# The lower part of a split weight tile, computed by GpSimd instead of VectorE (delta-rule attention feeding a softplus MLP)

## The chip, the core and the metric

The kernel runs on one core of one Trainium2 chip. The metric is the device time of one execution in microseconds; where several executions were timed, their median. The profiled execution is one of its own, with its own time. Engine names in the profile's rows: PE is TensorE (PEld its weight loads), DVE is VectorE, ACT is ScalarE, POOL is GpSimd, SP is SyncE, which here only issues DMAs.

## What is computed

Two layers, one after the other. The first is a delta-rule linear attention over 768 steps, for 4 batches of 8 heads with head size 48; the second a feed-forward layer over the resulting 3072 tokens, 384 -> 2048 -> 384, with a softplus between the two weight matrices:

```python
for t in range(S):                       # attention, per batch b and head h
    y[:, :, t] = einsum('bhd,bhde->bhe', q[:, :, t], state)
    v_old = einsum('bhde,bhd->bhe', state, kt)
    state = state + bt * einsum('bhd,bhe->bhde', kt, vt - v_old)
...
h = x @ w_in                             # feed-forward, x is y as 3072 x 384
g = maximum(h, 0) + log1p(exp(-abs(h)))
return g @ w_out
```

All inputs and outputs are float32, except that the weights arrive as 64-bit floating point words, read as pairs of 32-bit integers.

## The kernel before, in words

The sequence is cut into 12 steps of 64 positions (`NS`), and all 32 heads go through a step together. A step of the attention forms the Gram matrix of its keys, inverts a triangular system (`invert`, `finish`, `join`, `cross_a`, `arrange`, `cross_b`), and then gives the output of the step and the new state (`k_state`, `p_half`, `u_all`, `y_all`, `state`). The inverse is prepared for two steps at a time: `invert` is a long row of small VectorE instructions on the tiles Z, ltq and work (lines 199 to 229), `finish` transposes the result into the tile tt (lines 235 and 236), `join` (line 246 and behind) multiplies with tt, and `arrange` copies a part of tt (line 275) and clears it (line 277, a GpSimd memset).

The feed-forward layer (`moe`) follows one step behind: the 256 tokens of step s are called chunk s here. A chunk goes through the 16 column tiles f of the hidden layer in pairs. For a pair, TensorE multiplies the tokens with the first weights into ph (line 465), ScalarE computes Abs, Exp and Ln (469 to 471), VectorE puts the softplus together, and TensorE adds the pair's product with the second weights to po (line 448), one pair late: `late` holds that product back until the next pair's ph has been issued. ph has two buffers.

The precision differs by chunk. Chunk 0 uses plain float32 weights. From chunk 1 on every operand is split into an upper part in the type fp32r and a lower part, the difference to it, and three products are added (`TERMS`: upper x upper, upper x lower, lower x upper). The softplus is then made by three VectorE instructions: line 473 (its inputs are ph in PSUM and a in SBUF), line 475 (a cast, the upper part gh) and line 476 (a subtraction, the lower part gl).

The weights are prepared once. `weights` (lines 382 to 411) turns the 64-bit words into float32 with four VectorE instructions a tile (396, 399, 403, 406) and a ScalarE copy (409) into HF[f]. `split` (lines 413 to 419) then makes the two parts, once for each of the 16 tiles of 128 x 768 elements, and is called in chunk 1 just ahead of the pair that needs them: a ScalarE copy of HF[f] into hf, a tile from the three buffers of "ex" (line 416); a ScalarE cast of hf to the upper part w[:, 0] (line 418); and the difference of the two into the lower part w[:, 1] (line 419). W[f] has the place of HF[f]. The next user of an "ex" buffer waits until line 419 has read it.

The order on each engine is fixed when the program is built. The prologue's order is written out by hand (`manual_schedule`); after it a scheduler decides, from the order of the code and its own estimates of durations, in which order each engine gets its instructions. At run time every engine works its list in that order, and waits on semaphores for what it needs. SP's list of DMAs is not touched by what follows.

Of the kernel before, what the change touches and what calls it, by code (L numbers as in the profile page):

```python
# [12 lines left out]
ALU = mybir.AluOpType  # L13
# [22 lines left out]
def deltanet_moe(ctx, tc, kT, qT, kN, kI, vN, beta, wts, out):  # L36
    nc = tc.nc
# [375 lines left out]
    def split(f):  # L413

        hf = two.tile([P, 2 * DM], F32, name="ex", bufs=3)
        nc.scalar.copy(hf, HF[f])
        w = W[f] = one.tile([P, 2, 2 * DM], F32R, name=f"w{f}")
        nc.scalar.copy(w[:, 0], hf)
        nc.vector.tensor_tensor(w[:, 1], hf, w[:, 0], op=ALU.subtract)  # L419


    def moe():
# [4 lines left out]
        for s in range(NS):  # L427
# [26 lines left out]
            for f0 in range(0, NF, 2):  # L454
                while done[0] < f0 + 2:
                    next(conversion)
                if s == 1:
                    for f in range(0 if f0 == 0 else f0 + 2, min(f0 + 4, NF)):
                        split(f)
# [320 lines left out]
```

## Time and profile before

| | |
|---|---|
| runs of the kernel before | 673.43 us median of 3 (671.69 to 679.93) |
| the profiled execution | 672.51 us, of which 670.8 us is the span from its first to its last instruction |
| granted TensorE clock, mean | 0.971 |
| busy of the span | PE 91%, PEld 85%, DVE 67%, ACT 56%, POOL 5% |
| line 419, the instruction that moves | 16 times on DVE, 124.9 to 168.9 us, 15.1 us in all |

The span falls into three parts. Up to about 120 us come the loading of inputs, the first inverses and the conversion of the weights. From there to about 190 us chunk 1 runs, with the 16 splits in it. Behind that, 10 more chunks run with everything at hand, and TensorE works nearly without a break. Line numbers in rows (L419) are those of the code above; out<-in are the names of tiles, buffer numbers left out; "idle ... <-" names what ended the idle time just before the instruction.

### The profile page before, as it was taken

What the parts mean: (1) busy time and instruction counts of PE and PEld (TensorE: products, weight loads), DVE (VectorE), ACT (ScalarE), POOL (GpSimd) and SP (SyncE); (2) the same over time, 40 slices, a digit from 0 to 9 for tenths busy, and PEclk for the clock granted to TensorE, in tenths of its full rate; (3) what the DMA queues carried; (4) which work ended last, traced back from release to release, by engine and by line L of the source; (5) the groups of instructions that cost most, each with busy time, mean ns of one, the idle gap of its engine ahead of it and who ended that gap; (6) DMA issues with size and microseconds to landing.
All of it is one profiled execution on the core that took longest, in us unless ns stands there. A gap on an engine that the chain in (4) does not pass through costs nothing.

```text
span 670.8 us, 24090 instructions
## 1 busy us (share of the span) xinstructions
PE 612.4 (91%) x10736; PEld 571.7 (85%) x10736; DVE 451.9 (67%) x970; ACT 372.5 (56%) x687; POOL 30.5 (5%) x56
## 2 busy tenths in 40 slices
PE   4456968899888999989999999999999999999997
PEld 3455756579888999988999999998999998999997
DVE  4966498978555985556997558985539984544443
ACT  4334767879664447464456555555554546454433
POOL 3200010000000001000001000001000001000000
PEclk9998977899998999999999999997999998999999
DMA  9837286000140120140210322200302100200000
GB/s 232 271 98 207 64 262 150 0 25 4 52 108 26 48 61 26 50 108 27 70 38 28 81 78 71 61 25 21 90 4 71 38 24 5 60 25 13 2 23 23
DMA packets 35095, 44.80 MB, mean 67 GB/s; under 512 B 21776, under 2 KB 27184, under 8 KB 34992
## 3 DMA queue, kind: packets, MB, share of 16 engines
q1 hardware_dynamic: 34992, 43.27, 22.9%
q8 instruction: 84, 1.38, 0.9%
q14 instruction: 19, 0.16, 0.1%
HBM read 36.27 MB, written 4.72 MB: 61 GB/s over the span
## 4 chain that ended last, share of the span: by engine, by line
PE 77%; ACT 8%; DVE 7%; issue 5%; DMA 2%; POOL 1%; SPq 0%; ACTq 0%; DVEq 0%; POOLq 0%
PE ph L465 29%; PE po L448 27%; PE pa L345 4%; PE pa L304 3%; PE pa L330 2%; PE pa L318 2%; PE pa L284 2%; PE pa L131 2%; PE pa L294 2%; DMA big<-qT 1%; ACT tt L275 1%; PE pa L263 1%; PE pa L127 1%; DVE ex L406 1%; DVE ex L403 1%
## 5 line engine op out<-in xcount | busy, mean ns | idle before, releaser
L465 PE MATMUL ph<-x,w 128*128 128x256 f32 x1680 | 240.9, 294 | 2.2 <-DVE a L473 0.9
L465 PEld LDWEIGHTS ph<-x,w 128*128 128x128 f32 x1680 | 224.6, 192 | 10.1 <-DVE w L419 1.2
L448 PE MATMUL po<-w,gh 128*128 128x384 f32 x768 | 208.0, 357 | 3.7 <-DVE gh L479 2.4
L469 ACT ACTIVATE a<-ph 128x512 f32<-128x512 f32 x96 | 57.5, 599 | 171.7 <-PE ph L465 171.7
L448 PEld LDWEIGHTS po<-w,gh 128*128 128x128 f32 x768 | 135.0, 190 | 13.6 <-DVE gh L479 3.2
L473 DVE SCALAR_TENSOR_TENSOR a<-ph,a 128x512 f32<-128x512 f32 x88 | 60.5, 689 | 106.6 <-ACT a L471 106.2
L448 PE MATMUL po<-w,gl 128*128 128x384 f32 x352 | 119.2, 339 | 0.0
L448 PEld LDWEIGHTS po<-w,gl 128*128 128x128 f32 x352 | 66.3, 188 | 0.5 <-DVE gl L476 0.2
L476 DVE TENSOR_TENSOR gl<-a,gh 128x512 fp32r<-128x512 f32 x88 | 60.9, 692 | 2.9
L470 ACT ACTIVATE a<-a 128x512 f32<-128x512 f32 x96 | 60.9, 634 | 2.7
L471 ACT ACTIVATE a<-a 128x512 f32<-128x512 f32 x96 | 60.8, 634 | 2.3
L229 DVE TENSOR_TENSOR Z<-Z,work 128x84 f32<-128x84 f32 (+14 forms) x148 | 44.2, 306 | 2.8
L223 DVE TENSOR_TENSOR work<-Z,ltq 128x84 f32<-128x84 f32 (+14 forms) x148 | 44.2, 305 | 2.5
L475 DVE CAST gh<-a 128x512 fp32r<-128x512 f32 x88 | 37.7, 428 | 7.7 <-PE po L448 5.6
L311 DVE TENSOR_TENSOR big<-pa,maskP 64x512 f32<-64x512 f32 x44 | 30.2, 687 | 12.9 <-PE pa L304 12.4
L345 PEld LDWEIGHTS pa<-big 128*64 128x64 f32 x768 | 27.8, 150 | 10.9 <-ACT big L322 7.1
L345 PE MATMUL pa<-big 128*64 128x64 f32 x768 | 31.0, 238 | 6.7 <-ACT big L322 5.7
L322 ACT COPY big<-pa 64x384 f32<-64x384 f32 x46 | 21.7, 473 | 19.5 <-PE pa L318 18.7
L277 POOL MEMSET tt<- 32x512 f32 x24 | 13.1, 545 | 402.3 <-PE pa L263 224.9
L304 PE MATMUL pa<-big,kt 48*64 48x64 f32 x704 | 27.4, 229 | 3.4 <-issue 2.0
L304 PEld LDWEIGHTS pa<-big,kt 48*64 48x64 f32 x704 | 24.9, 144 | 4.0 <-issue 2.3
L333 ACT COPY big<-pa 48x384 f32<-48x384 f32 x44 | 20.9, 475 | 8.4 <-PE pa L330 7.9
(103 smaller groups left out, 645.1 us busy)
## 6 DMA issues: line engine op xcount, KB each, us to landing
w<-wts SPq DMA_DIRECT2D x16, 768.0 KB, 5.6
kt<-kT SPq DMA_DIRECT2D x24, 192.0 KB, 4.3
big<-qT SPq DMA_DIRECT2D x24, 192.0 KB, 4.1
nv<-vN SPq DMA_DIRECT2D x12, 384.0 KB, 4.2
ki<-kI SPq DMA_DIRECT2D x24, 192.0 KB, 3.6
out<-ex SPq DMA_DIRECT2D x24, 192.0 KB, 1.9
ka<-kN SPq DMA_DIRECT2D x8, 384.0 KB, 3.6
x<-x SPq DMA_DIRECT2D x66, 32.0 KB, 2.2
```

The lines of the kernel that those rows point to most:

```text
L223: nc.vector.tensor_tensor(tmp[:, a:a + r, 0:j], Z[:, a + j + 1:a + n, a + j:a + j + 1].to_broadcast([P, r, j]), lq[:, a + j:a + j + 1, a:a ...
L229: nc.vector.tensor_tensor(z, z, tmp[:, a:a + r, 0:j], op=ALU.add)
L304: nc.tensor.matmul(pt[tk[ab], i, :], kts[s % 3][dr[ab], 8 * g + i, :], bv[dr[ab], ab, 8 * g + i, 0:C], start=True, stop=True)
L345: nc.tensor.matmul(py[tk[ab], i, :], big[:, at + C:at + 2 * C], big[:, at:at + C], start=True, stop=True)
L448: nc.tensor.matmul(po[:, h, 0:DM], g[b][:, f - f0, h * P:(h + 1) * P], weight(f, a, DM, DM), start=(f == 0 and i == 0), stop=end)
L465: nc.tensor.matmul(ph[:, f - f0], weight(f, a, k * P, P), xr[b][k], start=(c == 0), stop=(c == len(terms1) * NK - 1))
L469: nc.scalar.activation(a, ph, AF.Abs)
L470: nc.scalar.activation(a, a, AF.Exp, scale=-1.0)
L471: nc.scalar.activation(a, a, AF.Ln, bias=1.0)
L473: nc.vector.scalar_tensor_tensor(a, ph, 0.0, a, op0=ALU.max, op1=ALU.add)
L475: nc.vector.tensor_copy(g[0], a)
L476: softplus[0] = nc.vector.tensor_tensor(g[1], a, g[0], op=ALU.subtract)
```

## The change

One line: the subtraction of line 419 is issued to GpSimd instead of VectorE. The operands, their types and the tile it writes are the same.

```diff
 def split(f):
         hf = two.tile([P, 2 * DM], F32, name="ex", bufs=3)
         nc.scalar.copy(hf, HF[f])
         w = W[f] = one.tile([P, 2, 2 * DM], F32R, name=f"w{f}")
         nc.scalar.copy(w[:, 0], hf)
-        nc.vector.tensor_tensor(w[:, 1], hf, w[:, 0], op=ALU.subtract)
+        nc.gpsimd.tensor_tensor(w[:, 1], hf, w[:, 0], op=ALU.subtract)
```

The scheduler orders the whole program anew, so rows move on other engines as well. Three places are shown; w_1765 and w_1770 are the split tiles of f = 0 and 1, w4_2082 and w5_2087 those of f = 4 and 5, and so on.

The first is VectorE's list at the end of the weight conversion, where the inverse for steps 2 and 3 begins (one piece of the difference):

```order
 L203 TENSOR_TENSOR ltq<-ltq,Z 128x16x16 x2
-L419 TENSOR_TENSOR w_1765<-ex,w_1765 128x768
 L403 SCALAR_TENSOR_TENSOR ex<-w_1618,ex 128x768
 L205 TENSOR_TENSOR Z<-ltq,cT 128x16x16
-L419 TENSOR_TENSOR w_1770<-ex,w_1770 128x768
 L406 SCALAR_TENSOR_TENSOR ex<-w_1618,ex 128x768
 L479 SCALAR_TENSOR_TENSOR gh<-ph,a 128x512
 L205 TENSOR_TENSOR Z<-ltq,cT 128x16x16
```

The subtractions of f = 0 and 1 leave the row ahead of line 479, the softplus of a pair of chunk 0; nothing takes their place.

The second is TensorE's list where chunk 1 comes to the third pair, f = 4 and 5; line 246 is the first product with the new inverse tt. Before:

```order
L465 MATMUL ph_2207<-x1_1326,w4_2082 128x256 x9
L465 MATMUL ph_2207<-x1_1326,w5_2087 128x256 x2
...
L448 MATMUL po_1762<-w1_1770,gl_1808 128x384
L465 MATMUL ph_2207<-x1_1326,w5_2087 128x256 x7
L246 MATMUL pa_1842<-tt_1832,x2_1643 32x16 x64
```

And with the change:

```order
L465 MATMUL ph_2207<-x1_1326,w4_2082 128x256 x2
...
L448 MATMUL po_1762<-w1_1770,gl_1808 128x384
L465 MATMUL ph_2207<-x1_1326,w4_2082 128x256 x7
L465 MATMUL ph_2207<-x1_1326,w5_2087 128x256 x2
L246 MATMUL pa_1842<-tt_1832,x2_1643 32x16 x64
L465 MATMUL ph_2207<-x1_1326,w5_2087 128x256 x7
```

Of each tile's nine products the third is the first that reads the lower part of the weights. The twelve products of line 448 for f = 0 and 1 now stand ahead of that third product of f = 4 instead of that of f = 5, and line 246 ahead of the third of f = 5.

The third is GpSimd's list with the change, from the thirteenth subtraction on; before, the four memsets of line 277 stood there alone, directly behind those of the previous inverse's mask (line 194):

```order
L419 TENSOR_TENSOR w12_2478<-ex_2476,w12_2478 128x768
L419 TENSOR_TENSOR w13_2483<-ex_2481,w13_2483 128x768
L277 MEMSET tt_1832 32x16x32 x2
L419 TENSOR_TENSOR w14_2624<-ex_2622,w14_2624 128x768
L419 TENSOR_TENSOR w15_2629<-ex_2627,w15_2629 128x768
L277 MEMSET tt_1832 32x16x32 x2
L194 AFFINE_SELECT Z_79<-ncT_2897 128x1024
```

The first two memsets are behind 14 subtractions, the other two behind all 16, and GpSimd's next instruction after them is the one of line 194 as before.

## The prediction

> **What bounds the kernel now.** I read the page's busy shares first, then the busy times by stage around the 16 splits, then TensorE's waits there, and last the timelines of single engines.
>
> ```profile
> span 670.8 us, 24090 instructions
> PE 612.4 (91%) x10736; PEld 571.7 (85%) x10736; DVE 451.9 (67%) x970; ACT 372.5 (56%) x687; POOL 30.5 (5%) x56
> ```
>
> TensorE is the busiest engine and GpSimd nearly idle. But the instruction that moves runs only from 124.9 to 168.9 us, so the stages there decide, not the shares:
>
> ```profile
> core 0: us, PE busy (x) PEld busy (x) DVE busy (x) ACT busy (x) POOL busy (x), PEclk, DMA share, GB/s
> 122.00:134.00 12.00, 11.61 (x37) 7.77 (x38) 12.00 (x33) 9.56 (x15) 0.00 (x0) 0.86 0.00 0
> 142.00:160.00 18.00, 16.28 (x342) 14.65 (x341) 17.83 (x33) 17.87 (x29) 0.00 (x0) 1.00 0.07 25
> 400.00:450.00 50.00, 50.00 (x536) 48.31 (x532) 42.90 (x100) 25.70 (x47) 0.00 (x0) 1.00 0.17 49
> ```
>
> The first two numbers of a row are the stage and its length. From 122 to 134 us VectorE has no free moment (12.00 of 12.00). From 142 to 160 us VectorE and ScalarE are both full (17.83 and 17.87 of 18.00) and TensorE misses 1.7 us. Later, as from 400 to 450 us, TensorE is full and nothing else matters: what TensorE loses or wins around the splits is carried to the end. So the question is how much of TensorE's idle time there hangs on VectorE. Its waits from 120 to 200 us (us in total, times, longest):
>
> ```profile
> PE po L448 <- DVE gh L479: 2.4, 2, 2.0
> PE ph L465 <- DVE a L473: 0.9, 1, 0.9
> PE ph L465 <- DVE w L419: 0.8, 2, 0.5
> PE po L448 <- DVE gh L475: 0.7, 1, 0.7
> ```
>
> The 2.0 us wait is over at 121.9 us, ahead of the first split's subtraction. What can hang on the moved instruction is the other 0.4, then 0.9, 0.8 and 0.7: 2.8 us. **More than 2.8 us (0.4%) can't be won.**
>
> **What the change removes.** 16 subtractions on VectorE:
>
> ```profile
> L419 DVE TENSOR_TENSOR w<-ex,w 128x768 fp32r<-128x768 f32 x16 | 15.1, 956 | 3.2 <-ACT w L418 3.2
> ```
>
> ```profile
> 123.77 0.53 DVE L399 TENSOR_SCALAR ex<-ex 128x768 int32<-128x768 int32 x1
> ...
> 124.87 0.96 DVE L419 TENSOR_TENSOR w<-ex,w 128x768 fp32r<-128x768 f32 x1
> 125.74 0.96 DVE L403 SCALAR_TENSOR_TENSOR ex<-w,ex 128x768 int32<-128x768 int32 x1
> ...
> 128.68 0.69 DVE L479 SCALAR_TENSOR_TENSOR gh<-ph,a 128x512 f32<-128x512 f32 x1
> ...
> 147.01 2.07 DVE L235 STREAM_TRANSPOSE tt<-Z 128x1024 f32<-128x1024 f32 x1
> ```
>
> One takes 0.96 us, and the next instruction starts 0.87 us after it (124.87 to 125.74): 0.87 us of VectorE's row are freed each time.
>
> **What one costs on GpSimd.** The trace has no GpSimd instruction with two tensor inputs. The nearest has one input of 768 elements, and the cheapest shows the fixed part:
>
> ```profile
> L617 POOL TENSOR_SCALAR_AFFINE_SELECT ki<-ki 48x768 f32<-48x768 f32 x2 | 2.2, 1080 | 0.1
> ...
> L596 POOL MEMSET half<- 128x1 f32 x1 | 0.1, 113 | 0.0
> ```
>
> If both inputs are read in one pass, 1.08 us is the lower bound; if each takes a pass, 2 x (1.08 - 0.11) + 0.11 = 2.05 us. I take 2.05 us, since an engine that is slower with one input than VectorE with two (1.08 against 0.96) hardly reads a second one for nothing. On the page GPSIMD Engine Reference, Performance versus the Vector engine, the Trainium skill gives 4497 ns for a two-input add of 2048 elements, an estimate of 1.69 us here; no run here shows it, and the sum below would be +0.4 us by it.
>
> **What it does to VectorE meanwhile.** This is the disputed part, and the trace has a place for it, at 17 to 21 us. First GpSimd, then VectorE:
>
> ```profile
> 15.04 0.96 POOL L194 TENSOR_SCALAR_AFFINE_SELECT Z<-ncT 128x256 f32<-128x256 f32 x2 [10.24 <-DVE ncT L183]
> ...
> 17.46 1.19 POOL L617 TENSOR_SCALAR_AFFINE_SELECT ki<-ki 48x768 f32<-48x768 f32 x1
> ...
> 19.49 0.97 POOL L617 TENSOR_SCALAR_AFFINE_SELECT ki<-ki 48x768 f32<-48x768 f32 x1
> ...
> 88.91 2.29 POOL L194 TENSOR_SCALAR_AFFINE_SELECT Z<-ncT 128x256 f32<-128x256 f32 x2 [10.72 <-DVE ncT L183]
> ```
>
> ```profile
> 16.96 0.43 DVE L203 TENSOR_TENSOR ltq<-ltq,Z 128x256 f32<-128x256 f32 x1
> ...
> 17.77 1.15 DVE L203 TENSOR_TENSOR ltq<-ltq,Z 128x256 f32<-128x256 f32 x1
> ...
> 19.50 0.98 DVE L223 TENSOR_TENSOR x<-Z,ltq 128x14 f32<-128x14 f32 x2
> 20.40 0.29 DVE L229 TENSOR_TENSOR Z<-Z,x 128x14 f32<-128x14 f32 x2
> ```
>
> The same VectorE instruction takes 0.43 us alone and 1.15 us when it starts inside a GpSimd instruction that runs until 18.65: held for 0.72 of 0.88 us, 82%. Two small ones take 0.98 instead of 0.29 us, held for 0.69 of 0.97 us, 71%. So a GpSimd instruction that reads SBUF holds VectorE's two-input instructions for about 77% of its time; GpSimd is held in turn: two instructions of line 194 take 0.96 us at 15.04, beside a transpose with one input, and 2.29 us at 88.91, beside lines 403 and 406. For a subtraction of 2.05 us that is 1.58 us held, more than the 0.87 us freed. That is the crux: **a subtraction on GpSimd can cost VectorE more time than it did on VectorE**, wherever VectorE has such an instruction next in its row.
>
> **Place one, 122 to 130 us.** Each subtraction starts when ScalarE's cast is done:
>
> ```profile
> 122.02 0.83 ACT L418 CAST w<-ex 128x768 fp32r<-128x768 f32 x1
> ...
> 124.50 0.82 ACT L418 CAST w<-ex 128x768 fp32r<-128x768 f32 x1
> ...
> 143.30 0.83 ACT L418 CAST w<-ex 128x768 fp32r<-128x768 f32 x1
> ```
>
> The first runs from 122.85 and holds to 124.43, so line 399, due at 123.77, is held 0.66 us. The second starts at 125.32, when VectorE is among lines 203 and 403: 1.58 us. Freed: 2 x 0.87 = 1.74. Line 479 comes 0.66 + 1.58 - 1.74 = 0.5 us later, and TensorE, which waits for it already, **0.5 us** later:
>
> ```profile
> 129.43 2.85 PE L448 MATMUL po<-w,gh 128*128 128x384 f32 x8 [0.39 <-DVE gh L479]
> ```
>
> The third cast stands behind line 409 on ScalarE, which waits for line 406, so it is out of this stretch.
>
> **Place two, 144 to 152 us.** TensorE before:
>
> ```profile
> 144.18 0.50 PE L465 MATMUL ph<-x,w 128*128 128x256 f32 x2
> 145.18 1.33 PE L465 MATMUL ph<-x,w 128*128 128x256 f32 x9 [0.49 <-DVE w L419]
> 146.35 0.51 PE L448 MATMUL po<-w,gh 128*128 128x384 f32 x2
> ...
> 148.46 0.99 PE L465 MATMUL ph<-x,w 128*128 128x256 f32 x7
> 149.38 1.26 PE L246 MATMUL pa<-tt,x 32*32 32x16 f32 x128
> 151.57 0.47 PE L465 MATMUL ph<-x,w 128*128 128x256 f32 x2 [0.93 <-DVE a L473]
> 152.34 1.33 PE L465 MATMUL ph<-x,w 128*128 128x256 f32 x9 [0.29 <-DVE w L419]
> ```
>
> It waits 0.49 + 0.93 + 0.29 = 1.7 us. The lower part of f = 4 arrives at 144.13 + 2.05 = 146.2 us instead of 145.1; that is hidden, since the new order puts the twelve products of line 448 (146.35 to 148.46: 2.1 us) ahead of its first reader. But those two subtractions hold the small instructions of the inverse's end, lines 223 and 229, which all have two inputs in SBUF: 2 x 1.58 - 1.74 = 1.4 us, and line 235, which ended at 149.08, ends at 150.5. Line 246 needs it. In the new order TensorE comes to line 246 after 0.5 + 2.1 + 0.8 + 0.3 us of work from 144.18, at 147.9, and waits 2.6 us; the old waits of 1.7 us lie behind other work then. Net **+0.9 to +1.0 us**.
>
> **Place three, 152 to 170 us.** The other ten subtractions. VectorE is left with the softplus (line 473 reads PSUM, lines 475 and 476 can be held), and ScalarE's list, unchanged in content, is full. One hold per pair delays gh or gl by 1.6 us, but their product stands a whole pair later on TensorE: nothing. If that cover were gone, five pairs would cost up to 5 x 1.6 = 8 us less the waits replaced. GpSimd itself is in time: the lower part of f = 13, the tenth from f = 4, is read at about 172.9 us, the twelfth product of the first row here:
>
> ```profile
> 171.44 1.95 PE L465 MATMUL ph<-x,w 128*128 128x256 f32 x15
> ...
> 177.78 1.03 PE L318 MATMUL pa<-nv,tt 64*64 64x48 f32 x30
> ```
>
> Up to (172.9 - 144.1) / 10 = 2.9 us each this costs nothing. The memsets of line 277 behind the subtractions are first needed by line 318 at 177.8 us, and the "ex" buffers are given back within a ScalarE split (two times 0.83 us and its softplus share). Both hidden on the same condition.
>
> **Sum.** +0.5 + 1.0 = +1.5 us on 672.5 us (span 670.8 and 1.7 around it): 674.0 us. The median of the runs is 673.4, 0.9 above that execution: **674.9 us**. A measurement of this kernel tells about 2% from no change, 13.5 us, so this is no change.
>
> **The rivals.** *Held for the whole instruction.* VectorE gets nothing in while GpSimd subtracts, 2.05 us each time: place one is 1.13 + 2.05 - 1.74 = +1.4 us, place two 4.1 - 1.74 = 2.4 us on line 235 and a wait of 3.6 - 1.7 = +1.9 us, together +3.3: 676.7 us. For it: 82% at 17.77. Against it: VectorE's instruction ended only 0.27 us after GpSimd's there, less than the 0.43 us that it needs. This is also the rule of the Trainium skill's page SBUF - State Buffer, Who interferes with whom: a shared port pair, locked for a whole instruction, so that the other "fully blocks". The trace agrees with it in kind and falls short in size.
>
> *No hold worth the name.* The freed 0.87 us arrive in full, and the 2.8 us of waits vanish: 670.6 us. For it: at 15.04 the two engines don't disturb each other. Against it: 17.77 and 19.50.
>
> *GpSimd becomes the bound.* A subtraction of 4.5 us (four passes rather than two, if the conversion to fp32r and being held add that much): f = 13 is ready at 144.1 + 45 = 189.1 instead of 172.9, TensorE stands 16.2 us, 689.6 us. It decides from 2.9 us on, and passes 2% at 4.2 us. For it: no row with an fp32r output on GpSimd, and 88.91 (1.15 us each instead of about 0.5) shows that GpSimd can double when it is held. Against it: twice my upper bound, though VectorE loses 16 instructions that could hold it.
>
> *It washes out.* ScalarE is as full as VectorE in place two, so its order, not VectorE's, sets line 473, and gain and loss cancel: 673.4 us. For it: 17.87 of 18.00.
>
> **How the numbers follow.** Forecast 0.42 (own range 673 to 676.5), held for the whole 0.15, no hold 0.2, washed out 0.14, GpSimd the bound 0.09. The range reaches down to the no-hold case with half a microsecond of spread, 670, and up to 681, where place three costs half its 8 us on top of the whole hold; beyond lies nearly only the bound case. Slower by over 2%: that case's larger part, 0.08. Faster by over 2% would need 13.5 us where 2.8 can be won: 0.01. Within 2%: 0.91.
>
> **What would show it.** Right: line 419 on POOL at 1.7 to 2.4 us each; VectorE rows of lines 399, 203, 223 at twice their time and more beside them; line 235 later against the casts of f = 4 and 5; TensorE idle before line 246; VectorE's busy total near 437 + the holds. Wrong: holds absent and TensorE without waits from 144 to 152 us (no hold), or line 465 waiting for POOL by name for many microseconds (the bound).

## The result, and the profile after

| | median, us | runs |
|---|---|---|
| before | 673.97 | 4 (671.69 to 679.93) |
| with the change | 683.84 | 4 (678.28 to 688.19) |
| ratio, with its 95% interval | **1.0106** | [1.0056, 1.0155] |

The change makes the kernel slower, by about 1%, and the time lies outside the predicted range (670 to 681). Here and below the ratio is an estimate from the fast runs alone, so it can differ from the quotient of the medians, which take in all runs. The profiled execution took 678.28 us. The page of the changed kernel, first its busy shares:

```profile
span 676.5 us, 24116 instructions
PE 614.6 (91%) x10736; PEld 575.0 (85%) x10736; DVE 449.9 (66%) x954; ACT 371.5 (55%) x687; POOL 59.7 (9%) x72
```

VectorE lost 16 instructions worth 15.1 us of busy time and is only 2.0 us less busy (451.9 before): the others became longer. The stages of the prediction, with the same columns:

```profile
122.00:134.00 12.00, 9.12 (x36) 6.51 (x35) 11.37 (x37) 7.37 (x13) 5.45 (x3) 1.00 0.00 1
142.00:160.00 18.00, 13.13 (x211) 11.70 (x213) 12.64 (x14) 15.30 (x24) 16.20 (x9) 0.72 0.04 13
```

From 142 to 160 us TensorE is busy for 13.1 us instead of 16.3, at a granted clock of 0.72 instead of 1.00, and GpSimd is busy for 16.2. Neither ScalarE (15.30) nor VectorE (12.64) is full any more. The moved instruction, on GpSimd (least, median and greatest duration in ns), and its first rows in the timeline:

```profile
L419 POOL TENSOR_TENSOR w<-ex,w x16: 1809/1824/2064, 119.6 to 170.3; 128x768 fp32r<-128x768 f32 x16
```

```profile
119.64 1.83 POOL L419 TENSOR_TENSOR w<-ex,w 128x768 fp32r<-128x768 f32 x1 [28.89 <-ACT w L418]
122.11 1.82 POOL L419 TENSOR_TENSOR w<-ex,w 128x768 fp32r<-128x768 f32 x1 [0.64 <-ACT w L418]
...
141.70 3.66 POOL L419 TENSOR_TENSOR w<-ex,w 128x768 fp32r<-128x768 f32 x2 [9.47 <-DVE Z L229]
```

Now VectorE's timeline beside them:

```profile
120.48 1.41 DVE L399 TENSOR_SCALAR ex<-ex 128x768 int32<-128x768 int32 x1
121.81 2.39 DVE L203 TENSOR_TENSOR ltq<-ltq,Z 128x256 f32<-128x256 f32 x2
...
141.72 1.93 DVE L223 TENSOR_TENSOR work<-Z,ltq 128x26 f32<-128x26 f32 x2
143.59 1.92 DVE L229 TENSOR_TENSOR Z<-Z,work 128x26 f32<-128x26 f32 x2
145.45 0.28 DVE L223 TENSOR_TENSOR work<-Z,ltq 128x14 f32<-128x14 f32 x2
...
147.85 1.98 DVE L236 STREAM_TRANSPOSE tt<-Z 128x1024 f32<-128x1024 f32 x1
...
150.49 1.42 DVE L475 CAST gh<-a 128x512 fp32r<-128x512 f32 x1
151.94 2.19 DVE L476 TENSOR_TENSOR gl<-a,gh 128x512 fp32r<-128x512 f32 x1
```

Read the two fences side by side. GpSimd works from 119.64 to 121.47; line 399 (0.53 us before) starts at 120.48, inside that, and ends 0.42 us after it, so it had to wait for the whole rest. The pair of line 203 ends 0.27 us after GpSimd's 123.93. Two subtractions stand back to back from 141.70 to 145.36: a pair of line 223, which takes 0.30 us, lasts until 143.65, one of line 229 until 145.51, and the next takes 0.28 us again. **VectorE gets one or two small instructions in between two subtractions, and otherwise stands for the whole of each.** A subtraction lengthens the VectorE rows beside it by 1.63 us (2.39 instead of 0.76 for line 203, 1.93 instead of 0.30 for line 223). It isn't only those with two inputs: lines 399 and 475 have one (150.49 us: 1.42 instead of 0.43 us for line 475). The transpose of line 236 is not longer for it (1.98 us), nor is line 473, which reads PSUM.

TensorE pays. Its waits from 115 to 205 us (total, times, longest):

```profile
PE po L448 <- DVE gh L479: 4.7, 2, 2.9
PE pa L246 <- issue: 1.5, 1, 1.5
PE pa L246 <- DVE tt L235: 1.4, 1, 1.4
PE po L448 <- DVE gl L476: 1.2, 1, 1.2
PE po L448 <- DVE gh L475: 1.2, 1, 1.2
PE po L448 <- ACT ex L451: 1.1, 1, 1.1
```

No wait of TensorE names GpSimd: the subtractions are in time. All but two of these name VectorE's results. The 1.1 us for line 451, ScalarE's copy of po, is also there in e10, e12 and e13 below, which have the same order on TensorE: it comes with the order. In TensorE's timeline they stand at the prediction's places one and two and where three begins:

```profile
118.61 2.85 PE L448 MATMUL po<-w,gh 128*128 128x384 f32 x8 [1.77 <-DVE gh L479]
...
126.93 2.85 PE L448 MATMUL po<-w,gh 128*128 128x384 f32 x8 [2.88 <-DVE gh L479]
...
141.68 0.50 PE L465 MATMUL ph<-x,w 128*128 128x256 f32 x2
...
148.06 1.26 PE L246 MATMUL pa<-tt,x 32*32 32x16 f32 x128 [1.35 <-DVE tt L235]
149.25 1.51 PE L465 MATMUL ph<-x,w 128*128 128x256 f32 x7
151.96 1.01 PE L448 MATMUL po<-w,gh 128*128 128x384 f32 x2 [1.21 <-DVE gh L475]
154.18 0.69 PE L448 MATMUL po<-w,gl 128*128 128x384 f32 x1 [1.21 <-DVE gl L476]
154.67 0.84 PE L448 MATMUL po<-w,gh 128*128 128x384 f32 x2
...
159.60 1.38 PE L253 MATMUL pa<-x,tt 32*32 32x16 f32 x128
...
174.35 1.26 PE L253 MATMUL pa<-x,tt 32*32 32x16 f32 x128
```

From 150 us on the products themselves are longer: two of line 448 take 0.84 us where the prediction's rows have 0.51. That is the clock, 0.50 from 149.7 to 159.9 us.

### The profile page after: what moved, and what is told of

Its sections match the earlier page's. It is cut to its first block, busy times and chain, and to the rows that moved or that the text cites. A ratio compares the mean times of both kernels' runs of the same rounds, so it can differ in the third digit from the quotient of the medians.

```text
span 676.5 us, 24116 instructions
## 1 busy us (share of the span) xinstructions
PE 614.6 (91%) x10736; PEld 575.0 (85%) x10736; DVE 449.9 (66%) x954; ACT 371.5 (55%) x687; POOL 59.7 (9%) x72
## 3 DMA queue, kind: packets, MB, share of 16 engines
q8 instruction: 84, 1.38, 0.9%
## 4 chain that ended last, share of the span: by engine, by line
PE 75%; DVE 10%; ACT 5%; issue 5%; DMA 3%; POOL 1%; SPq 0%; ACTq 0%; DVEq 0%; POOLq 0%
PE ph L465 28%; PE po L448 27%; PE pa L345 4%; PE pa L304 3%; PE pa L330 2%; PE pa L318 2%; PE pa L284 2%; PE pa L294 2%; DVE ex L403 1%; DMA big<-qT 1%; DVE ex L406 1%; PE pa L131 1%; ACT tt L275 1%; PE pa L263 1%; DVE tt L236 1%
## 5 line engine op out<-in xcount | busy, mean ns | idle before, releaser
L448 PEld LDWEIGHTS po<-w,gh 128*128 128x128 f32 x768 | 136.4, 192 | 20.0 <-DVE gh L479 8.3
L448 PE MATMUL po<-w,gl 128*128 128x384 f32 x352 | 120.9, 343 | 1.2 <-DVE gl L476 1.2
L476 DVE TENSOR_TENSOR gl<-a,gh 128x512 fp32r<-128x512 f32 x88 | 63.8, 725 | 3.2 <-DVE Z L229 0.2
L229 DVE TENSOR_TENSOR Z<-Z,work 128x84 f32<-128x84 f32 (+14 forms) x148 | 47.4, 327 | 2.8
L223 DVE TENSOR_TENSOR work<-Z,ltq 128x84 f32<-128x84 f32 (+14 forms) x148 | 46.3, 320 | 2.5
L419 POOL TENSOR_TENSOR w<-ex,w 128x768 fp32r<-128x768 f32 x16 | 29.5, 1855 | 51.0 <-ACT w L418 40.5
```

The lines of the kernel that those rows point to most:

```text
L223: nc.vector.tensor_tensor(tmp[:, a:a + r, 0:j], Z[:, a + j + 1:a + n, a + j:a + j + 1].to_broadcast([P, r, j]), lq[:, a + j:a + j + 1, a:a ...
L229: nc.vector.tensor_tensor(z, z, tmp[:, a:a + r, 0:j], op=ALU.add)
L448: nc.tensor.matmul(po[:, h, 0:DM], g[b][:, f - f0, h * P:(h + 1) * P], weight(f, a, DM, DM), start=(f == 0 and i == 0), stop=end)
L476: softplus[0] = nc.vector.tensor_tensor(g[1], a, g[0], op=ALU.subtract)
```

## The experiments

Three theories stood at the start. **H**: GpSimd, reading its two operands, holds VectorE's instructions between tiles in SBUF for its whole duration; TensorE waits for them, and its clock falls behind the waits. **L**: the lower parts, or the "ex" buffers, come later, since 1.82 us is twice 0.96. **O**: the scheduler's new order is worse, whoever subtracts. The kernel before was timed again beside each group, 23 to 29 runs with medians from 675.56 to 677.14 us; ratios are to these. Unless a diff says otherwise, the edit is at line 419 of the changed kernel and the scheduler orders the program anew.

### e1: GpSimd as busy, almost without reading

```diff
-        nc.gpsimd.tensor_tensor(w[:, 1], hf, w[:, 0], op=ALU.subtract)
+        for k in "rwwr":
...
+                X["p"] = nc.gpsimd.tensor_tensor(w[:, 1, 0:8], hf[:, 0:8], w[:, 0, 0:8], op=ALU.subtract) if k == "r" else nc.gpsimd.memset(w[:, 1].bitcast(F32), 2.0 ** -14)
```

A subtraction of 8 columns, two fills of the whole lower part, and 8 columns again, one after the other (the left out line only fixes that order). The lower parts are constants.

> GpSimd keeps its place in every split but hardly reads: two subtractions of 8 columns (they wait for ScalarE's cast and hold the ex buffer) around two memsets of the whole lower tile. The lower weight parts are therefore a constant instead of the difference. GpSimd is meant to be busy about as long per split as with the subtraction (1.8 us in the trace of the change), and TensorE's order at the third pair is the one of the change. Theory H (a reading GpSimd holds VectorE's two-input instructions for its whole duration, TensorE then waits and its clock falls): no holds longer than 0.3 us on VectorE, the clock at 1.00 from 140 to 172 us, ratio to before 0.995 to 1.003. Theory L (the lower part comes about a microsecond later and the buffers with it): nothing changes against the change, ratio 1.009 or more. Theory O (the scheduler's new order is what costs): the same, 1.009 or more.

Measured: 673.48 us median of 10, ratio 0.9942 [0.9899, 0.9985]. GpSimd is about as busy (13.1 us from 142 to 160 us, 16.2 with the change), and the loss has turned into a gain. Lateness of the lower part (L) does not cost anything here; that the reading matters (H) stands. Against H's expectation the clock was 0.81 from 160 to 172 us, behind a wait of 1.9 us for line 475. The order is not the change's throughout, so O is not settled by this run.

### e2, e3, e6, e7: only some of the sixteen on GpSimd

```diff
-        nc.gpsimd.tensor_tensor(w[:, 1], hf, w[:, 0], op=ALU.subtract)
+        eng = nc.gpsimd if f < 4 else nc.vector      # e2; e3: f >= 4; e6: f in (4, 5); e7: f > 5
+        eng.tensor_tensor(w[:, 1], hf, w[:, 0], op=ALU.subtract)
```

> Only the subtractions of f = 0 to 3 on GpSimd, the other twelve on VectorE. Theory H: TensorE's wait for line 479 near 125 us grows from 0.4 to about 2.9 us, the stage from 142 to 160 us looks as before; +2 to +3 us, ratio 1.002 to 1.006. Theory L: nothing reads these lower parts before 137 us, so 0, ratio 0.998 to 1.002. Theory O: the order of the first pairs is hardly touched, 0.

> Only the subtractions of f = 4 to 15 on GpSimd. Theory H: lines 223, 229, 475 and 476 held beside them, the clock at half for some 10 us between 145 and 172 us, +5 to +8 us, ratio 1.007 to 1.012. Theory L: TensorE waits for the lower parts by name (line 465 after POOL line 419), +3 us or more. Theory O: +5 us or more, and the same if the subtractions were elsewhere.

> Only the subtractions of f = 4 and 5 on GpSimd: the place where the prediction put 1.0 us. Theory H with the prediction's split (the hold of the inverse's end is what counts): line 235 later against the casts by 1.5 to 2 us, ratio 1.001 to 1.004. The rival split (the ten subtractions behind it count, since line 475 and 476 are held where TensorE needs gh and gl at once): below 1.001.

> Only the subtractions of f = 6 to 15 on GpSimd: the place where the prediction put 0. With the prediction's split: ratio 0.998 to 1.001. With the rival split: TensorE's waits for lines 475 and 476 of about 1.2 us each and its clock at half behind them, ratio 1.002 to 1.006.

| | on GpSimd | median, us | ratio |
|---|---|---|---|
| e2 | 4 | 677.01 of 10 | 0.9998 [0.9957, 1.0040] |
| e3 | 12 | 679.69 of 10 | 1.0044 [1.0003, 1.0086] |
| e6 | 2 | 682.22 of 6 | 1.0105 [1.0057, 1.0153] |
| e7 | 10 | 678.92 of 12 | 1.0038 [1.0006, 1.0069] |

This missed what H expected for e2 and e3 (both lower) and for e6 (higher). The loss is no sum over subtractions: e6 and e7 together would make 1.43%, and e3, which has just their twelve subtractions, makes 0.44%. The intervals of e3 and e6 overlap, so which of the two costs more is not told. e7 lies where the rival split was expected: the ten subtractions that the prediction put at nothing cost something, and TensorE waits 3.1 us for line 475 in two pieces. Each of these kernels also has an order of its own, so the number on GpSimd is not the only thing that differs.

### e4: more work on VectorE, none on GpSimd

```diff
-        nc.gpsimd.tensor_tensor(w[:, 1], hf, w[:, 0], op=ALU.subtract)
+        nc.vector.tensor_tensor(w[:, 1], hf, w[:, 0], op=ALU.subtract)
+        nc.vector.tensor_tensor(hf, hf, w[:, 0].bitcast(F32), op=ALU.subtract)
```

The second line repeats the subtraction; nobody reads its result.

> All subtractions on VectorE as before, and behind each a second one of the same size whose result nobody uses (it overwrites the ex buffer). VectorE loses 16 x 0.87 us more, as it would lose about 0.95 us per split by being held 1.82 us for 0.87 freed; the lower part comes as early as before; GpSimd does nothing. Theory H, in the form that VectorE's lost time is the cost: +5 to +10 us, ratio 1.007 to 1.015, with gaps on TensorE from 122 to 134 and 144 to 160 us. Theory L: 0 to +2 us, ratio below 1.003.

Measured: 684.72 us median of 4, ratio 1.0127 [1.0048, 1.0205]. Taking time from VectorE in this stretch is enough for a loss of the change's size. The second line also keeps the "ex" buffer longer and gives the kernel an order of its own, so the run is a hint and no proof.

### e5: the change once more

> The change itself once more, beside the other parts on one chip, since f = 0 to 3 alone gave 0 and f = 4 to 15 alone 3 us where both together were put at 7 us (3.8 to 10.4). Theory H: line 419 at 1.8 us on POOL, no VectorE instruction with two inputs in SBUF ending inside it, TensorE's clock below 0.85 in 142 to 160 us; ratio 1.004 to 1.010. If the parts simply add, 1.003 to 1.006; if the first result was the better estimate, 1.008 or more.

Measured: 683.71 us median of 6, ratio 1.0106 [1.0063, 1.0149].

### e8: the change, with TensorE kept busy in its gaps

```diff
-                            c += 1
+                            c += 1; [nc.tensor.matmul(po[:, 0, 0:DM], W[0][:, 0, 0:P], W[1][:, 0, 0:DM], start=False, stop=False) for _ in range(6 if s == 1 and f == 5 and c == 2 else 0)]
...
-                    end = f == NF - 1 and i == k - 1
+                    end = f == NF - 1 and i == k - 1; [nc.tensor.matmul(po[:, 0, 0:DM], W[0][:, 0, 0:P], W[1][:, 0, 0:DM], start=False, stop=False) for _ in range(6 if s == 1 and f == 2 and h == 0 and i in (0, 2) else 0)]
```

18 products that nobody needs are added into po in chunk 1.

> The change, with 18 products of 128 x 384 that nobody needs put on TensorE in chunk 1, twelve ahead of and among the first products of f = 2 and six ahead of the third product of f = 5, so that it has work in the gaps near 146 to 156 us (they add products of weights to chunk 1's sums, so chunk 1's output differs). They are 18 x 0.17 = 3.1 us of work. If TensorE's clock falls because of the gaps, and the clock costs about as much as the gaps themselves: the clock near 1.00 from 142 to 172 us, and 1 to 4 us less than the change in spite of the added work. If the gaps alone cost and the clock is chance: 0 to 3 us more than the change, and the clock as low as there.

Measured: 684.22 us median of 12, ratio 1.0111 [1.0077, 1.0146]; the granted clock was 0.81 from 142 to 160 us and 1.00 from 160 to 172 (0.72 and 0.78 with the change). The time is the change's. The products may have filled gaps, or won on the clock what they cost; the run does not tell these apart.

### e9, e10, e11: the order and the subtraction's engine, each by itself

After the whole program is recorded, and before the scheduler runs, each instruction of TensorE, VectorE, ScalarE and GpSimd but the sixteen gets an edge to its predecessor in a written list. The edge fixes the order and waits for nothing.

```diff
     run(mg)
+    pin(tc, mybir)
...
+def pin(tc, mybir):
+    named = {i.name: i for i in tc.nc.cur_bb.bb.instructions}
+    info = mybir.DependencyInfo(mybir.DependencyClass.NoSync, mybir.DependencyReason.DATA)
+    for runs in ORDER.values():
+        names = [f"I-{n + j}" for n, k in runs for j in range(k)]
+        for a, b in zip(names, names[1:]):
+            tc.add_manual_dep(named[b], a, info, reason="issue_after")
```

e9 is the changed kernel with the list of the kernel before, e10 the kernel before with the list of the changed one, e11 the kernel before with the list of e6.

> All sixteen subtractions on GpSimd, as in the change, but TensorE, VectorE, ScalarE and GpSimd issue everything else in exactly the order of the kernel before (an edge without a wait from each instruction to its predecessor there). If the loss is GpSimd holding VectorE whatever the order, this keeps it: 1.006 to 1.011. If the loss is the scheduler's new order, it is gone: 0.996 to 1.002. In between: each has a part.

> All sixteen subtractions on VectorE, as before, but the four engines issue everything else in exactly the order of the change. Nothing holds VectorE. If the loss is GpSimd holding VectorE: 0.998 to 1.003. If the loss is the new order, which brings some products forward on TensorE because the scheduler counts VectorE as free: 1.006 to 1.011.

> All sixteen subtractions on VectorE; the four engines issue everything else in exactly the order of the kernel with only f = 4 and 5 on GpSimd, which was as slow as the change (1.0105). If its order made that loss: 1.006 to 1.011. If the two held stretches made it: 0.998 to 1.003.

| | subtraction on VectorE | on GpSimd |
|---|---|---|
| order of before | 1 | e9: **1.0087** [1.0056, 1.0118] |
| order of the change | e10: **1.0051** [1.0019, 1.0084] | 1.0106 (e5: [1.0063, 1.0149]) |

Each costs something by itself. The hold, in the old order, makes 0.87%; the new order, with VectorE still subtracting, 0.51%, between the two ranges expected for e10; together they make 1.06%, which the intervals tell neither from the sum of 1.38% nor from the 0.87% alone. (e5 was timed in another group than e9 and e10, each beside its own runs of the kernel before.) e11 is at 1.0032 [1.0003, 1.0061], below what its order was expected to make if it explained e6 (1.0105).

Where e9 loses is seen row by row, since its order is that of the kernel before. TensorE before (rows not shown yet), then e9:

```profile
121.90 4.46 PE L448 MATMUL po<-w,gh 128*128 128x384 f32 x8 [2.02 <-DVE gh L479]
...
156.54 1.26 PE L253 MATMUL pa<-x,tt 32*32 32x16 f32 x128
```

```profile
122.61 4.54 PE L448 MATMUL po<-w,gh 128*128 128x384 f32 x8 [2.02 <-DVE gh L479]
...
132.55 4.54 PE L448 MATMUL po<-w,gh 128*128 128x384 f32 x8 [2.81 <-DVE gh L479]
...
149.03 0.50 PE L465 MATMUL ph<-x,w 128*128 128x256 f32 x2
150.93 1.34 PE L465 MATMUL ph<-x,w 128*128 128x256 f32 x9 [1.40 <-POOL w L419]
...
155.55 1.26 PE L246 MATMUL pa<-tt,x 32*32 32x16 f32 x128 [0.35 <-DVE tt L235]
...
163.10 1.26 PE L253 MATMUL pa<-x,tt 32*32 32x16 f32 x128
...
175.00 1.26 PE L253 MATMUL pa<-x,tt 32*32 32x16 f32 x128
```

From the first row to the two products of line 465: 22.28 us before (121.90 to 144.18), 26.42 in e9, 4.1 more. The wait for line 479 grew from 0.39 to 2.81 us (2.4), and the eight products behind it took 4.54 instead of 2.85 us (1.7): the granted clock was 0.50 from 133.1 to 136.5 us. On to line 246: 5.20 before, 6.52 in e9, 1.3 more. On to line 253: 7.16 and 7.55, 0.4 more. To the next line 253, through place three: 11.90 and 11.90, nothing. The sum is 5.8 us; the medians differ by 6.0 (681.55 and 675.56). VectorE's rows behind the wait of 2.81 us are lines 399, 203 and 205. The last takes 0.41 us when it isn't held, and is held by the third subtraction, which with the change starts only behind line 479. GpSimd's row, then VectorE's:

```profile
128.21 2.52 POOL L419 TENSOR_TENSOR w<-ex,w 128x768 fp32r<-128x768 f32 x1 [0.29 <-ACT w L418]
```

```profile
129.00 2.02 DVE L205 TENSOR_TENSOR Z<-ltq,cT 128x256 f32<-128x256 f32 x1
...
149.07 3.65 DVE L223 TENSOR_TENSOR work<-Z,ltq 128x26 f32<-128x26 f32 x2
```

The last row is a pair that takes 0.30 us by itself. It stands through two subtractions (149.05 to 152.68): here only one instruction got in between them.

Now the order by itself, TensorE in e10:

```profile
120.29 4.54 PE L448 MATMUL po<-w,gh 128*128 128x384 f32 x8 [2.01 <-DVE gh L479]
...
142.57 0.51 PE L465 MATMUL ph<-x,w 128*128 128x256 f32 x2
...
147.62 1.25 PE L246 MATMUL pa<-tt,x 32*32 32x16 f32 x128
...
151.08 0.62 PE L448 MATMUL po<-w,gh 128*128 128x384 f32 x2 [1.18 <-DVE gh L475]
153.39 0.69 PE L448 MATMUL po<-w,gl 128*128 128x384 f32 x1 [1.70 <-DVE gl L476]
...
158.81 1.26 PE L253 MATMUL pa<-x,tt 32*32 32x16 f32 x128
...
170.62 1.26 PE L253 MATMUL pa<-x,tt 32*32 32x16 f32 x128
```

Place one is as before (22.28 us). But between lines 246 and 253 there are now waits for lines 475 and 476, 1.18 and 1.70 us: in the new order TensorE comes to that product earlier than VectorE, which still has the subtractions, is done with gh and gl (e12 and e13 below show the same order without these waits).

### e12, e13: exactly the change's order, with less to read

Order pinned to the list of the change, and at line 419 of the changed kernel:

```diff
-        nc.gpsimd.tensor_tensor(w[:, 1], hf, w[:, 0], op=ALU.subtract)
+        nc.gpsimd.memset(w[:, 1].bitcast(F32), 2.0 ** -14)                            # e12
+        nc.gpsimd.tensor_scalar(w[:, 1], hf, 2.0 ** -12, None, op0=ALU.mult)          # e13
```

> All four engines issue everything in exactly the order of the change; each of the sixteen subtractions on GpSimd is one fill of the whole lower part with 2^-14, which reads nothing (the lower parts are constants, and the fill waits for no split). If the loss is that GpSimd's reading holds VectorE: the gain of a freed VectorE shows, 0.990 to 0.998, and VectorE's instructions beside the fills take their usual times. If the new order costs by itself, even with VectorE free: 1.003 to 1.008.

> The same exact order; each of the sixteen subtractions on GpSimd is one product of the unsplit tile with 2^-12, which reads one operand from on-chip memory instead of two (the lower parts are a scaled copy, and do not wait for the upper part). If any reading by GpSimd holds VectorE for the whole instruction: 1.004 to 1.011, with VectorE's two-input instructions beside it at 1.4 us and more. If only an instruction with two such operands holds it: as the fill, 0.990 to 0.998.

Measured: e12 676.65 us median of 12, ratio 1.0020 [0.9991, 1.0049], between its two expected ranges; e13 675.91 us median of 12, ratio 0.9973 [0.9935, 1.0010], inside the second of its own. In one and the same order on TensorE, VectorE and ScalarE, the subtraction costs 1.06%, and neither the fill nor the one-operand product costs anything that the intervals show. It isn't for being shorter: the product takes 2.14 us in the median against 1.82. Both also leave out the wait for the cast of line 418; e1 keeps it, and loses nothing either. GpSimd in e13 (least, median and greatest duration in ns, then a row of the timeline), then VectorE:

```profile
L419 POOL TENSOR_SCALAR w<-ex x16: 2127/2144/4897, 119.9 to 166.3; 128x768 fp32r<-128x768 f32 x16
```

```profile
122.85 9.35 POOL L419 TENSOR_SCALAR w<-ex 128x768 fp32r<-128x768 f32 x3 [0.78 <-ACT ex L416]
```

```profile
122.91 0.77 DVE L203 TENSOR_TENSOR ltq<-ltq,Z 128x256 f32<-128x256 f32 x2
123.58 0.97 DVE L403 SCALAR_TENSOR_TENSOR ex<-w,ex 128x768 int32<-128x768 int32 x1
...
127.58 0.31 DVE L223 TENSOR_TENSOR work<-Z,ltq 128x36 f32<-128x36 f32 x2
127.81 0.92 DVE L229 TENSOR_TENSOR Z<-Z,work 128x36 f32<-128x36 f32 x2
```

All of these stand beside a busy GpSimd. Line 203 takes 0.77 us for two, as long as in e12 beside fills (0.74), where the change has 2.39; only now and then is a group held for about 0.6 us (0.92 instead of 0.31). The 4.90 us are the first of the three products from 122.85, beside this dense row of VectorE: there GpSimd is the one that takes longer. In e12 and e13 neither the waits for lines 475 and 476 nor that for line 235 occurs. TensorE in e12:

```profile
145.18 1.26 PE L246 MATMUL pa<-tt,x 32*32 32x16 f32 x128
...
150.71 1.26 PE L253 MATMUL pa<-x,tt 32*32 32x16 f32 x128
```

The stretch from line 465 (x2) over line 246 to line 253 takes 4.97 + 5.53 us in e12; with the change 6.38 + 11.54.

| TensorE, from - to, us | change | e5 | e10, VectorE | e13, one operand | e12, fill |
|---|---|---|---|---|---|
| first row of line 448 - line 465 x2 | 23.07 | 23.05 | 22.28 | 20.53 | 20.51 |
| - line 246 | 6.38 | 6.38 | 5.05 | 4.97 | 4.97 |
| - line 253 | 11.54 | 11.50 | 11.19 | 6.01 | 5.53 |
| - next line 253 | 14.75 | 11.81 | 11.81 | 15.22 | 13.99 |

All five have one order, so each line of the table is the same work. e13 and e12 give some of their lead back in the last line, where they wait for line 473 (2.4 and 1.8 us) and fall to half clock too. TensorE's 2001st to 4001st matmul took 127.8 us before, 132.0 in e9, 129.2 in e10, 134.9 and 134.3 with the change, 128.4 in e13 and 127.6 in e12: most of the difference arises there in e9 and with the change, less than half of it in e10. These are single executions.

## Why the prediction was wrong, by its own steps

- **The most to be won, 2.8 us.** Not contradicted: without a hold, e1 gained 3.9 us (0.9942 of 675 us or so, interval 1 to 7), e13 1.8 and e12 lost 1.4, neither told from nothing.
- **2.05 us for a subtraction.** 1.82 us, within the bounds. The reason given for the upper one is not borne out: the one-operand product of e13 needs 2.14 us, more than the subtraction with two. The estimate of 1.69 us, from the Trainium skill's page GPSIMD Engine Reference, Performance versus the Vector engine, is 7% below the trace.
- **The hold, 77% of GpSimd's time, 1.58 us.** Wrong as a mechanism, and nearly right in size by luck: a share that was too small of a time that was too long. Measured are 1.63 us, and the hold lasts until the subtraction's end. The rows at 17 to 21 us say so too: VectorE's instructions end there 0.27 and 0.02 us behind GpSimd's. The prediction took the 0.27 us as speaking against a whole hold, but line 203 ends 0.27 us behind GpSimd with the change as well. So the rival "held for the whole instruction" had the mechanism, with a chance of 0.15; it too has nothing at place three. The rule of the Trainium skill's page SBUF - State Buffer, Who interferes with whom, that the pair is locked for a whole instruction, agrees with the trace for the subtraction (1.93 instead of 0.30 us for line 223), but not for e13's product, which reads too (0.77 us for line 203).
- **Place one, +0.5 us.** In the change's order +0.8 (23.07 against 22.28): right. In the old order it is 4.1 (e9), since a third subtraction holds VectorE ahead of line 479 there (the wait is 2.4 us longer) and the clock fell behind the wait (1.7).
- **Place two, +0.9 to +1.0 us, by a wait of 2.6 us at line 246.** The prediction has line 246 at 6.3 us behind the two products of line 465 (150.5 less 144.18); it came at 6.38, and 1.3 us later than in e10, in the same order. Right in place and size, but the wait at line 246 itself is 1.35 us: another 1.09 us had already gone to line 451, which the prediction does not name.
- **Place three, nothing, since gh and gl have a whole pair's cover.** This is the step of the sum that failed. From line 246 to line 253 the change takes 11.54 us, where the same order takes 5.53 with the fill and 6.01 with the product: 5.5 to 6.0 us where the prediction has none. The cover was lost to the new order, which brings the product of line 448 forward on TensorE: before, the first eleven products of the next pair stand ahead of it (151.57 and 152.34 in the prediction's rows), with the change none. What then fills the gap is a busy VectorE. With the change it is the hold (line 475 takes 1.42 and line 476 2.19 us), in e10 VectorE's own subtractions (waits of 1.18 and 1.70 us, 11.19 us for the stretch, and a kernel 0.51% slower). In e9, in the old order, the two stretches of place three cost 0.4 us and nothing, as good as written. The prediction quoted two moved pieces of the order and priced them with the old places of the rest; it named the loss of that cover, 8 us for five pairs, and held it for unlikely. It came in one pair, and most of its price was the clock.
- **No term for the clock.** This belongs to the same step. Of the 6.0 us that the change loses to e12 between lines 246 and 253 the two waits make 2.4; the remaining 3.6 are the same products at half clock. In e9 eight products behind a wait of 2.81 us took 4.54 instead of 2.85 us. The clock is no cause by itself: e9 has a granted clock of 1.00 from 142 to 182 us and loses 0.87% all the same, and e12 and e13 have 0.72 from 160 to 172 us and lose nothing that the intervals show.
- **The starting point.** The 674.9 us were built on a median of three runs, 673.43. Later groups of 23 to 29 runs of the same kernel lie at 675.6 to 677.1, so some 2 of the 8.9 us between prediction and result may be that. As a share, 0.2% was forecast (1.5 us) and 1.06% measured.
- **The rivals "GpSimd the bound" and "washes out"** did not happen: TensorE waits for GpSimd by name only in e9 (1.40 us), and the ratio's interval excludes 1.

**What stays open:** why two subtractions on GpSimd (e6) are as slow as sixteen. Its order alone makes 0.32% (e11; the two intervals just touch), and in one profile of each TensorE's 2001st to 4001st matmul took 134.9 us in e6 and 135.4 in e11, so the difference is not there. Whether e8's products won anything on the clock is open too, and so is what it is in the subtraction that holds VectorE: e13 differs from it in the number of operands and in the kind of instruction.

## What to carry to other kernels

An instruction moved to an idle GpSimd can still cost VectorE its time. For a subtraction of two operands in SBUF, count its whole duration as lost to the VectorE instructions between SBUF tiles beside it (transposes were not held), here 1.82 us against 0.87 us freed. Where a scheduler decides the order, it will place consumers as early as its estimate of the freed engine allows; look at every moved consumer, not only at those near the edit, and pin the order to price the two effects apart. Take the baseline from many runs before working out a difference of 1%.

## What the runs showed of the hardware that was not expected

- The one-operand product on GpSimd is slower (2.14 us for 128x768, fp32r out) than the two-operand subtraction (1.82 us), and hardly holds VectorE (now and then some 0.6 us); the subtraction holds it until its end. The one-operand instruction of line 617 also held VectorE to its end (two rows at 17 to 21 us before), so the number of operands alone does not decide. A fill of the same tile takes 0.74 us.
- Several subtractions in a row let VectorE through between two of them: one or two small instructions, then another stop of 1.8 us.
- TensorE falls to half clock for some microseconds behind waits that are each below 3 us (0.50 from 149.7 to 159.9 us with the change, behind waits of 1.09 and 1.35). On the page TensorE: Matmul & The Clock Gate, Part 1: The HAM clock gate, the Trainium skill has the clock halve after an idle window of about 3.4 us. No single idle time here is that long, and a wait of 2.88 us at 126.93 with the change left the eight products behind it at full clock (2.85 us), where one of 2.81 us in e9 did not (4.54 us). In all fifteen traces the granted clock keeps a value for a multiple of 3.41 us (10.24 us at half with the change, 3.41 in e9), so where a wait falls in that grid may decide; no run tests it.
